# Backward chain of a segment-recurrent attention block: the order strings of a four-step block rewritten

## The chip, the cores and the metric

The kernel runs on one core of a Trainium2 chip. A core has five engines that run their own streams of instructions side by side: TensorE (PE; matrix products, its weight loads shown as PEld), VectorE (DVE), ScalarE (ACT), GpSimd (POOL) and SyncE (SP). Engines wait for each other on semaphores. DMA transfers are issued by SyncE and by GpSimd here, each on a queue of its own, and are carried out by 16 DMA engines. The metric is the device time of one execution in microseconds (us).

## The reference

```python
x = A_x
xn = _layernorm(x, axis=-1)
return x + _A_ref(xn, A_mem0, A_Wq, A_Wk, A_Wv, A_Wo, A_seg_len) + _B_ref(xn, ...)
```

`_B_ref` is a two-layer network with a squared ReLU (512 to 1792 to 512). `_A_ref` is attention with a recurrent memory: 2048 rows in 64 segments of 32, 32 heads of 128, and 8 memory rows that are put ahead of each segment:

```python
for s in range(n_seg):
    xs = x[:, s * seg_len:(s + 1) * seg_len, :].copy()
    h = jnp.concatenate([mem, xs], axis=1)
    q = jnp.einsum('btd,dhe->bhte', h, Wq)
    ...
    scores = jnp.einsum('bhqe,bhke->bhqk', q, k) * scale
    scores = jnp.where(mask[None, None], scores, -1000000000.0)
    p = _softmax(scores, axis=-1)
    o = jnp.einsum('bhqk,bhke->bhqe', p, v)
    o = jnp.einsum('bhte,hed->btd', o, Wo)
    mem = o[:, :M, :].copy()
    outs.append(o[:, M:, :])
```

The kernel returns this output and, for a given gradient of it, the gradients of x, of the first memory and of all weights and biases: `_out, _vjp = jax.vjp(_f, ...)`, then `_vjp(grad_out)`. Since the memory of a segment is the first 8 rows of the one before, both directions are chains of 64 steps. What can be computed for all segments at once is done ahead of the chains or behind them.

## The kernel before

The stages follow one another: the network B and the projections that need no memory (to about 265 us), the forward chain (to about 1110), the backward work on the memory's rows that can be done together (to about 1350), the backward chain (to about 2310), and the weights' gradients. The diff touches only the backward chain, L1150 to L1174.

**A step of the backward chain.** Step by step from the last segment to the first, the gradient of the memory, GT, comes in and the gradient for the segment before goes out. In the names of the order strings, with 0 and 1 (or a and b) for the two halves of the heads:

- `o0mm`, `o1mm`: products of GT with Wo (L425); `o0ev`, `o1ev`: ScalarE copies to gON; `o0fl`, `o1fl`: transposes on TensorE (L166); `o0te`, `o1te`: VectorE copies to gOT.
- `vp`: products for the gradient of v (L1381, L1383), copied by `vea`, `veb` (rows of the segment, gv) and `vla`, `vlb` (memory rows, b_gvL). `s0`, `s1`: the scores' gradients (L470), whose softmax backward is `d1` to `d4` on VectorE, ending in gS (L588); `tu` transposes it to gST (L488).
- `kp` (from gS with b_qN and b_qNL) and `qp` (from gST with b_kN and b_kNL), both L629, write the same PSUM banks b_pp, half 0 and half 1 in banks of their own. Their copies are `kea`, `keb` into gk, `qea`, `qeb` into gq, `kla`, `klb` into b_gkL. `vp` and the tile b_T of the step's end use b_pp too.
- `vg`, `kg`, `qg`: products of these copies with Wv, Wk, Wq (L498), 16 matrix products each, summed in ps_gR. `ra` (ScalarE) and `rb` (VectorE) copy the sum to R, `ta`, `tb` transpose it (L534), `Ha`, `Hb` reduce it to the next GT and `xa`, `xb` to b_XT (L543).

**A block.** Four steps are a block (128 rows), and 16 blocks make the chain. What is done once a block has the prefix `L.`: loads of the next block's memory rows (`ldv`, `ldk`, `ldt`, `lq`, `gl`), the left products `G`, `H`, `I` (L1248, 8 matrix products each, twelve a block) that turn the memory rows' gradients, and the stores. The large ones are six of 512 KB, gv, gk and gq in two halves each: `vo0`, `vo1`, `ko0`, `ko1`, `qo0`, `qo1`, all from L1235 to S_GB. `sx`, `sl`, `gst`, `vst`, `kst`, `qst` are smaller ones, and `vtr`, `ktr`, `qtr`, `L.vtr`, `gs` transposing DMAs. The tiles G4 of gv, gk, gq have one buffer: a copy of the next block's step into such a tile waits until the store has read it.

**Who issues.** SyncE issues the stores, the transposing DMAs and the two halves `ldk0`, `ldk1` of b_kNL (L1334; they do something only once a block). GpSimd issues `ldp` (b_P, L1324), `ldq` (b_qN, L1331), `ldn` (b_kN, L1332), `ldv`, `ldk`, and between them copies the probabilities into PD (`pb`, L1329) and b_vl into b_vT (`vc`, L1343). Loads and `pb`, `vc`, `vtr` serve the step after the one in which they are named.

**The order.** It is written out by hand. `B_ORDER` has four strings, rows 0 to 3, one for each step of a block, and `play` walks through them block after block:

```python
k = nm.rstrip("+-")
lag = nm.count("-") - nm.count("+")
if k.startswith("L."):
    b = n - 1 - lag
...
    s = n * SPB + j - lag
    if 0 <= s < NSEG:
        steps[step(s)][k]()
```

A name with four plus signs belongs to the step of its row, with three to the step before, with five to the one after. `L.` names with one plus belong to the block just finished or under way, with two to the next, without one to the one before. Each engine executes its share of the names in the order in which they stand. Which engine makes which copy is set by `ENGS` (L1175): ScalarE makes `kea0`, `keb0`, `keb1`, `kla0`, `kla1`, `qea0`, `qea1`, `qeb0`, `ra` and the copies of o and v, VectorE `kea1`, `klb0`, `klb1`, `qeb1` and the gOT copies.

Large stores and loads near the block's boundary stand on SyncE in the order `vo0 vo1 ldk0 ldk1 ko0 qo0 qo1 sx vtr ko1`, all in row 0.

Of the kernel before, what the change touches and what calls it, by code (L numbers as in the profile page):

```python
# [26 lines left out]
def kernel(  # L27
# [35 lines left out]
    L = M + SEG  # L63
# [145 lines left out]
    with sb("p1b", 2) as p1b, sb("p1", 1) as p1:  # L209
# [90 lines left out]
        for rb in range(NRB):  # L300
# [38 lines left out]
            xb = xq[rb]  # L339
# [314 lines left out]
    def on_engines(act, vec):  # L654

        return dict([(n, acp) for n in act.split()] + [(n, vcp) for n in vec.split()])
# [332 lines left out]
    with sb("la", 2) as la, sb("ls", 2) as ls, sb("lo", 1) as lo_, sb("wg", 2) as wg, psum("lpp", 1) as lpp, psum("lr", 4) as lr:  # L989
# [158 lines left out]


    B_ORDER = (  # L1150
# [6 lines left out]
        "pb+++ rb+++ ldq+++ L.H2+ ta+++ tb+++ vc+++ Ha+++ Hb+++ o0mm++++ o0ev++++ o1mm++++ o1ev++++ xb+++ o0fl++++ "  # L1157
# [4 lines left out]
        "ra++++ L.G3+ rb++++ ta++++ Ha++++",  # L1162
# [5 lines left out]
        "ta++++ rb++++ Ha++++ tb++++ Hb++++",  # L1168
# [5 lines left out]
        "ta++++ L.qst+ kla1++++ tb++++ L.H0++ Ha++++ Hb++++")  # L1174
    ENGS = on_engines(  # L1175
        "L.ra0 kea0 keb0 keb1 kla0 kla1 o0ev o1ev qea0 qea1 qeb0 ra vea veb vla vlb",
        "kea1 klb0 klb1 o0te o1te qeb1")
# [499 lines left out]
```

## Time and profile before

| | |
|---|---|
| time, median of 3 runs | 2895.26 us (2886.53 to 2903.46) |
| the profiled execution's own time | 2894.31 us |
| its span, first to last instruction | 2892.5 us |
| mean granted TensorE clock | 0.975 |
| busy: PE / PEld / DVE / ACT / POOL | 93% / 50% / 44% / 35% / 23% of the span |
| DMA | 586.62 MB, mean 203 GB/s |

Each group of instructions in the profile has its line, engine, operation, the tile written and the tile read, how often it ran, its busy time and mean duration in ns, and behind the bar the idle time of the engine just ahead of it with what ended it ("releaser"). L numbers are lines of the kernel. "SPq" and "POOLq" are the times in which SyncE or GpSimd issued a DMA. The chain of waits is followed back from the last instruction to what released it at each step. "issue" is time in which an engine waited for nothing that the profile shows. In views by stretches, PEclk is the clock that the throttle granted to TensorE (1.00 is full speed), and the DMA share is the mean busy share of the 16 DMA engines.

### The profile page before, as it was taken

What the parts mean: (1) busy time and instruction counts of PE and PEld (TensorE: products, weight loads), DVE (VectorE), ACT (ScalarE), POOL (GpSimd) and SP (SyncE); (2) the same over time, 40 slices, a digit from 0 to 9 for tenths busy, and PEclk for the clock granted to TensorE, in tenths of its full rate; (3) what the DMA queues carried; (4) which work ended last, traced back from release to release, by engine and by line L of the source; (5) the groups of instructions that cost most, each with busy time, mean ns of one, the idle gap of its engine ahead of it and who ended that gap; (6) DMA issues with size and microseconds to landing.
All of it is one profiled execution on the core that took longest, in us unless ns stands there. A gap on an engine that the chain in (4) does not pass through costs nothing.

```text
span 2892.5 us, 114613 instructions
## 1 busy us (share of the span) xinstructions
PE 2677.7 (93%) x51115; PEld 1444.8 (50%) x51252; DVE 1277.4 (44%) x3754; ACT 1003.8 (35%) x2330; POOL 658.9 (23%) x1279
## 2 busy tenths in 40 slices
PE   7998999999999887988999889998989899999999
PEld 3444555555555555455555445554544444444444
DVE  4543566666665664443545445544544401000000
ACT  2323444444454445332433333333333301111111
POOL 1000000000000001223434333343334334322221
PEclk9998999999999999998999999999999999999999
DMA  9766599999999888987568867776777799999993
GB/s 251 262 203 171 133 218 205 223 218 220 222 213 209 205 207 202 273 240 196 155 171 199 200 162 177 174 221 170 175 164 178 246 285 228 203 201 236 202 212 82
DMA packets 841920, 586.62 MB, mean 203 GB/s; under 512 B 639713, under 2 KB 729330, under 8 KB 838098
## 3 DMA queue, kind: packets, MB, share of 16 engines
q1 hardware_dynamic: 800370, 455.50, 69.6%
q0 software_dynamic: 41056, 123.77, 14.8%
q8 instruction: 402, 6.59, 1.0%
q14 instruction: 92, 0.75, 0.1%
HBM read 184.95 MB, written 248.79 MB: 150 GB/s over the span
## 4 chain that ended last, share of the span: by engine, by line
PE 72%; DMA 9%; SPq 8%; DVE 5%; issue 4%; ACT 2%; POOL 0%; DVEq 0%; ACTq 0%; POOLq 0%
PE ps_proj L425 15%; PE ps_gw L1638 12%; PE ps_gR L498 11%; PE ps_R L498 5%; SPq L1518 4%; PE ps_tr L166 3%; PE ps_RL L1248 3%; PE b_pp L629 3%; PE ps_L L383 3%; DMA S_GB<-gk 2%; PE ps_sc L470 2%; PE ps_B L344 2%; PE ps_gxb L353 2%; PE f_pp L629 2%; PE f_T L534 2%
## 5 line engine op out<-in xcount | busy, mean ns | idle before, releaser
L1638 PE MATMUL ps_gw<-gn,HNc 128*128 128x512 bf16 x1883 | 416.5, 380 | 6.9 <-issue 3.2
L1638 PEld LDWEIGHTS <-HNc 128*128 128x128 bf16 x1920 | 188.1, 98 | 230.0 <-issue 7.7
L407 ACT CAST f_N<-ps_proj 128x512 bf16<-128x512 f32 x320 | 183.8, 581 | 200.7 <-PE ps_proj L425 183.7
L1571 ACT CAST wt<-ps_gw 128x512 bf16<-128x512 f32 x128 | 74.4, 587 | 450.0 <-PE ps_gw L1638 416.6
L425 PEld LDWEIGHTS <-X 128*32 128x32 bf16 x5760 | 143.1, 96 | 136.7 <-DVE X L543 21.1
L1554 DVE TENSOR_TENSOR gx<-ps_rows,gb 128x512 f32<-128x512 f32 x16 | 11.1, 691 | 429.2 <-PE ps_rows L1552 400.6
L887 POOL COPY kM<-f_kT 128x256 bf16<-128x256 bf16 x64 | 25.7, 402 | 738.0 <-DVE f_kT L410 563.4
L498 PE MATMUL ps_gR<-Wv,gv 128*32 128x512 bf16 x2048 | 143.9, 401 | 3.8 <-issue 3.8
L498 PE MATMUL ps_gR<-Wk,gk 128*32 128x512 bf16 (+1 forms) x2048 | 139.8, 384 | 6.4 <-DVE gk L410 4.6
L1638 PE MATMUL ps_gw<-GOc,gn 128*128 128x512 bf16 x626 | 138.4, 379 | 5.1 <-ACT wt L1571 3.1
L498 PE MATMUL ps_R<-Wo,OT 128*32 128x256 bf16 x4096 | 131.3, 282 | 1.3 <-DVE OT L410 1.1
L498 PE MATMUL ps_gR<-Wq,gq 128*32 128x512 bf16 (+1 forms) x2048 | 125.6, 357 | 6.3 <-issue 6.3
L407 ACT CAST gON<-ps_proj 128x512 bf16<-128x512 f32 x128 | 75.0, 586 | 158.0 <-PE ps_proj L425 158.0
L425 PE MATMUL ps_proj<-Wq,X 128*32 128x512 bf16 x1920 | 126.8, 380 | 1.4 <-issue 0.8
L425 PE MATMUL ps_proj<-Wo,GT 128*32 128x512 bf16 x2048 | 123.4, 382 | 3.9 <-DVE GT L1293 3.6
L1572 POOL DMA_DIRECT2D out_dram<-wt x120 | 64.8, 542 | 271.0 <-ACT wt L1571 258.1
L407 ACT CAST gk<-b_pp 128x256 bf16<-128x256 f32 x192 | 69.2, 379 | 165.2 <-PE b_pp L629 94.0
L425 PE MATMUL ps_proj<-Wk,X 128*32 128x512 bf16 x1920 | 124.4, 381 | 1.9 <-issue 1.3
L425 PE MATMUL ps_proj<-Wv,X 128*32 128x512 bf16 x1920 | 121.5, 378 | 0.0
L1324 POOL DMA_DIRECT2D b_P<-S_A x63 | 33.8, 537 | 378.2 <-issue 137.4
L1329 POOL COPY PD<-b_P 32x320 bf16<-32x320 bf16 x256 | 115.3, 451 | 8.6
L498 PEld LDWEIGHTS <-OT 128*32 128x32 bf16 x4096 | 106.8, 99 | 8.9 <-DVE OT L410 1.3
(285 smaller groups left out, 5266.4 us busy)
## 6 DMA issues: line engine op xcount, KB each, us to landing
S_A<-f_N SPq DMA_DIRECT2D x64, 512.0 KB
out_dram<-wt POOLq DMA_DIRECT2D x134, 128.0 KB, 5.3
S_A<-f_N SPq DMA_DIRECT2D x64, 256.0 KB
S_GB<-gv SPq DMA_DIRECT2D x32, 512.0 KB
S_GB<-gk SPq DMA_DIRECT2D x32, 512.0 KB
S_GB<-gq SPq DMA_DIRECT2D x32, 512.0 KB
b_kN<-S_A POOLq DMA_DIRECT2D x63, 256.0 KB, 4.5
b_qN<-S_A POOLq DMA_DIRECT2D x63, 256.0 KB, 3.7
```

Source lines behind the costliest of these rows:

```text
L166: nc.tensor.transpose(ps_ap, in_ap, ident[base:base + k, base:base + k])
L383: nc.tensor.matmul(ps[:], lhsT=x(dc), rhs=Wqkv[t][:, dc, c0:c0 + 512], start=(dc == 0), stop=(dc == DC - 1))
L407: nc.scalar.copy(out, in_)
L425: nc.tensor.matmul(o, lhsT=hT[:, dc, :], rhs=x, start=(dc == 0), stop=(dc == DC - 1), tile_position=(0, 32 * g))
L498: nc.tensor.matmul(R[32 * g:32 * g + 32, 0:(cs.stop - cs.start) * P].rearrange("p (a b) -> p a b", b=P), lhsT=XT(k, g), rhs=x[:, cs, :], s ...
L629: nc.tensor.matmul(o, lhsT=N_[32 * g:32 * g + m, kk * P:(kk + 1) * P], rhs=X(kk)[32 * g:32 * g + m], start=(i == 0), stop=(i == len(jobs) ...
L1248: nc.tensor.matmul(ps["R", i][32 * g:32 * g + 32, :].rearrange("p (a b) -> p a b", b=P), lhsT=B_[n][:, k, g, :], rhs=W(g * KH + k), start= ...
L1329: nc.gpsimd.tensor_copy(PD[32 * g:32 * g + 32, g], C["P"][32 * g:32 * g + 32, :, KW - L:KW])
L1518: nc.sync.dma_start_transpose(got[i][q][:, x, :].rearrange("p (k e) -> p k e", k=KH), S_GB[4 * q + x, t][:, g].rearrange("p k r -> p (k r)"))
L1571: nc.scalar.copy(wt[:], ps[:])
L1572: eng(dst, wt[:])
L1638: nc.tensor.matmul(ps[:], lhsT=l(rc), rhs=r(rc), start=(n == 0), stop=(n == RC_ALL - 1))
```

## The change

All four strings of `B_ORDER` are rewritten. The set of names and the engine of each copy are the same. On SyncE, the order of a block becomes `vo0 qo0` (end of row 3), `gst vo1 ko1 ko0 vtr ldk0 ktr ldk1 qo1` (row 0), `vtr sl kst sx` (row 1), `vtr L.vtr gs vst gl qtr ldt` (row 2), `vtr qst lq` (row 3). On GpSimd `ldq` for a block's first step moves to the end of row 3. Products, copies and reductions stand in other places too. TensorE's order in row 2, for example, is `kp0 vg1 qp0 I3 kg0 kp1 qp1 qg0 kg1 qg1 H3 ta tb` before and `kp0 qp0 vg1 kg0 kp1 qg0 qp1 kg1 qg1 ta` after.

```diff
--- before.py
+++ after.py
@@ -1148,30 +1148,30 @@
 
 
     B_ORDER = (
-        "L.vo0+ o0mm++++ o1mm++++ L.vo1+ o0ev++++ pb+++ xa+++ L.xt ldk0+++ o1ev++++ o0fl++++ xb+++ L.ra0+ vp0++++ "
-        "o0te++++ L.G2+ ldk1+++ vea++++ s0++++ d10++++ o1fl++++ d20++++ L.ko0+ d30++++ vla++++ o1te++++ vp1++++ "
-        "ldn+++ L.I1+ L.G1+ d40++++ ldp++++ ldq+++ veb++++ s1++++ d11++++ vlb++++ kp0++++ ldp+++++ vg1++++ L.qo0+ "
-        "tu0++++ L.qo1+ keb0++++ d21++++ qp0++++ kla0++++ L.sx+ vg0++++ kea0++++ d31++++ qeb0++++ d41++++ vtr++++ "
-        "L.ko1+ kg0++++ klb0++++ tu1++++ qp1++++ ldn++++ qeb1++++ qea0++++ qg0++++ qea1++++ kp1++++ qg1++++ keb1++++ "
-        "kea1++++ kg1++++ klb1++++ kla1++++ ra++++",
-        "pb+++ rb+++ ldq+++ L.H2+ ta+++ tb+++ vc+++ Ha+++ Hb+++ o0mm++++ o0ev++++ o1mm++++ o1ev++++ xb+++ o0fl++++ "
-        "vp0++++ xa+++ o0te++++ vla++++ s0++++ o1fl++++ vp1++++ d10++++ vea++++ vtr++++ d20++++ L.H1+ o1te++++ L.ktr+ "
-        "d30++++ d40++++ veb++++ vlb++++ tu0++++ vtr+++++ s1++++ d11++++ d21++++ ldp+++++ d31++++ vg0++++ kp0++++ "
-        "qp0++++ d41++++ vg1++++ qea0++++ qeb0++++ qg0++++ keb0++++ L.kst+ tu1++++ kla0++++ klb0++++ kp1++++ kea0++++ "
-        "kea1++++ kg0++++ qp1++++ keb1++++ kla1++++ qeb1++++ L.ra1+ L.I2+ kg1++++ qea1++++ L.ra2+ qg1++++ klb1++++ "
-        "ra++++ L.G3+ rb++++ ta++++ Ha++++",
-        "vc+++ tb+++ Hb+++ ldq+++ o0mm++++ xb+++ o1mm++++ o0ev++++ o0fl++++ pb+++ xa+++ o1ev++++ o0te++++ vp0++++ "
-        "s0++++ d10++++ vea++++ d20++++ o1fl++++ L.vtr+ vp1++++ o1te++++ vg0++++ vla++++ s1++++ d30++++ d40++++ "
-        "d11++++ L.sl ldn+++ veb++++ tu0++++ d21++++ vlb++++ kp0++++ keb0++++ vg1++++ d31++++ d41++++ L.vst+ L.gs+ "
-        "kea0++++ qp0++++ tu1++++ qea0++++ klb0++++ kla0++++ L.I3+ kg0++++ qeb0++++ kp1++++ L.gl++ qp1++++ ldp+++++ "
-        "qea1++++ kea1++++ keb1++++ qeb1++++ qg0++++ klb1++++ kla1++++ L.gst+ kg1++++ ldq++++ qg1++++ ra++++ L.H3+ "
-        "ta++++ rb++++ Ha++++ tb++++ Hb++++",
-        "o0mm++++ o1mm++++ o0ev++++ vc+++ L.ra3+ ldn+++ xb+++ vtr++++ o1ev++++ xa+++ L.ldt++ o0fl++++ pb+++ vp0++++ "
-        "vc++++ o1fl++++ o0te++++ s0++++ vea++++ vla++++ o1te++++ d10++++ d20++++ vp1++++ s1++++ d30++++ veb++++ "
-        "vlb++++ d40++++ d11++++ vg0++++ kp0++++ L.tb+ kla0++++ tu0++++ d21++++ qp0++++ vg1++++ d31++++ keb0++++ "
-        "d41++++ kea0++++ kg0++++ kp1++++ L.qtr+ qeb0++++ tu1++++ L.G0++ klb0++++ qp1++++ L.ldv++ L.ta+ qea0++++ "
-        "qg0++++ qeb1++++ kea1++++ keb1++++ qea1++++ kg1++++ L.lq++ klb1++++ qg1++++ L.I0++ ra++++ L.ldk++ rb++++ "
-        "ta++++ L.qst+ kla1++++ tb++++ L.H0++ Ha++++ Hb++++")
+        "L.xt o0mm++++ o1mm++++ ldn+++ L.G2+ o0ev++++ xb+++ o1ev++++ o0fl++++ L.gst vp0++++ L.vo1+ L.ko1+ xa+++ "
+        "o0te++++ vc+++ vp1++++ o1fl++++ veb++++ L.ko0+ s0++++ vtr++++ o1te++++ d10++++ L.H0+ L.H2+ ldk0+++ vla++++ "
+        "d20++++ vea++++ d30++++ vg1++++ d40++++ s1++++ d11++++ kp0++++ vg0++++ tu0++++ vlb++++ qp0++++ L.ra0+ "
+        "kla0++++ klb0++++ d21++++ L.ktr+ d31++++ keb0++++ ldk1+++ d41++++ vc++++ kea0++++ L.I2+ ldp++++ L.qo1+ "
+        "kg0++++ ldn++++ L.I1+ qeb0++++ qea0++++ tu1++++ qp1++++ qea1++++ qg0++++ qeb1++++ kp1++++ keb1++++ kea1++++ "
+        "kla1++++ qg1++++ kg1++++ ra++++ klb1++++",
+        "L.G1+ pb+++ ldq+++ rb+++ ta+++ Ha+++ tb+++ Hb+++ ldp++++ o0mm++++ o0ev++++ vtr++++ xa+++ o1mm++++ xb+++ "
+        "o0fl++++ o1ev++++ vp0++++ o0te++++ L.H1+ s0++++ vea++++ d10++++ o1fl++++ vp1++++ o1te++++ veb++++ vg0++++ "
+        "vc++++ d20++++ vla++++ vlb++++ s1++++ d30++++ d40++++ tu0++++ L.sl kp0++++ d11++++ qp0++++ d21++++ vg1++++ "
+        "kla0++++ kea0++++ qea0++++ L.kst+ d31++++ qeb0++++ L.G3+ d41++++ L.ra1+ tu1++++ keb0++++ L.I3+ qg0++++ "
+        "qp1++++ kp1++++ kg0++++ qea1++++ klb0++++ keb1++++ L.sx+ kla1++++ kea1++++ ldq++++ klb1++++ L.ra2+ qeb1++++ "
+        "kg1++++ qg1++++ ra++++ L.H3+ ta++++",
+        "rb+++ pb+++ Ha+++ tb+++ Hb+++ ldn+++ xa+++ vtr++++ o0mm++++ o1mm++++ xb+++ L.vtr+ L.ra3+ L.gs+ o0ev++++ "
+        "o0fl++++ o0te++++ L.vst+ o1ev++++ vp0++++ s0++++ d10++++ ldp++++ d20++++ o1fl++++ d30++++ vla++++ vea++++ "
+        "o1te++++ vp1++++ d40++++ tu0++++ vlb++++ vg0++++ s1++++ veb++++ vc++++ ldp+++++ d11++++ kp0++++ kea0++++ "
+        "klb0++++ qp0++++ kla0++++ d21++++ d31++++ qeb0++++ vg1++++ keb0++++ qea0++++ d41++++ tu1++++ kg0++++ L.gl++ "
+        "kp1++++ L.qtr+ qg0++++ kla1++++ qp1++++ L.ldt++ ldq++++ keb1++++ kea1++++ kg1++++ qeb1++++ qea1++++ qg1++++ "
+        "klb1++++ ldn++++ ra++++ ta++++ rb++++",
+        "tb+++ Ha+++ Hb+++ o0mm++++ xb+++ o0ev++++ vtr++++ xa+++ o1mm++++ pb+++ vp0++++ o0fl++++ o1ev++++ o1fl++++ "
+        "vea++++ o0te++++ s0++++ L.qst+ vla++++ o1te++++ vp1++++ d10++++ d20++++ d30++++ s1++++ d40++++ vg0++++ "
+        "vlb++++ tu0++++ L.lq++ veb++++ kp0++++ L.vo0++ qp0++++ qea0++++ d11++++ klb0++++ keb0++++ qeb0++++ kea0++++ "
+        "d21++++ kla0++++ L.G0++ d31++++ d41++++ vg1++++ L.ta+ L.ldv++ kp1++++ kg0++++ kea1++++ pb++++ kla1++++ "
+        "qg0++++ keb1++++ tu1++++ qp1++++ klb1++++ L.ldk++ qea1++++ kg1++++ qeb1++++ qg1++++ L.I0++ ldq++++ ra++++ "
+        "ta++++ rb++++ L.qo0++ L.tb+ Ha++++ tb++++ Hb++++")
     ENGS = on_engines(
         "L.ra0 kea0 keb0 keb1 kla0 kla1 o0ev o1ev qea0 qea1 qeb0 ra vea veb vla vlb",
         "kea1 klb0 klb1 o0te o1te qeb1")
```

## The prediction

> **What bounds the kernel now.** I read the chain of waits by engine first, then the backward chain's step times, then its waits, then one block's queues. In the page's chain:
>
> ```profile
> PE 72%; DMA 9%; SPq 8%; DVE 5%; issue 4%; ACT 2%; POOL 0%; DVEq 0%; ACTq 0%; POOLq 0%
> ```
>
> TensorE is the bound wherever it isn't kept waiting. The edit changes only the backward chain; the tile GT, whose last reduction ends a step, dates it, and a view by stretches shows one block and the first step of the next:
>
> ```profile
> L543 DVE TENSOR_REDUCE GT<-b_T x120: 223/225/226, 1400.9 to 2277.6; 128x16 bf16<-128x64 f32 x120
> ...
> core 0: us, PE busy (x) PEld busy (x) DVE busy (x) ACT busy (x) POOL busy (x), PEclk, DMA share, GB/s
> 1829.20:1847.90 18.70, 15.80 (x373) 8.13 (x374) 7.31 (x26) 6.03 (x16) 5.19 (x11) 0.91 0.87 256
> 1847.90:1860.90 13.00, 12.88 (x357) 7.14 (x357) 7.88 (x23) 5.35 (x15) 4.68 (x9) 1.00 0.60 112
> 1860.90:1873.90 13.00, 12.81 (x350) 7.06 (x349) 6.32 (x21) 5.63 (x15) 4.48 (x9) 1.00 0.70 134
> 1887.90:1905.50 17.60, 14.07 (x373) 7.58 (x373) 7.26 (x25) 6.13 (x16) 5.70 (x12) 1.00 0.97 307
> 1400.90:2277.60 876.70, 801.37 (x21074) 435.26 (x21078) 427.57 (x1341) 332.24 (x900) 335.07 (x652) 0.97 0.75 184
> ```
>
> Two reductions a step make 60 steps, 876.7/60 = 14.6 us each. The two middle rows are steps without disturbance: 13.00 us, TensorE busy for 12.88 and 12.81. Anything that stops TensorE there lengthens the step by as much. The rows of 18.70 and 17.60 are the first steps of a block, over which the DMA share is 0.87 and 0.97. Over the whole stretch TensorE stands for 876.7 - 801.4 = 75 us, and a mean clock of 0.97 is worth another 0.03 x 877 = 26 us. The waits of this stretch (us in total, times, longest) name a part of that:
>
> ```profile
> PE b_pp L629 <- issue: 27.7, 21, 3.9
> ACT gk L407 <- DMA S_GB<-gk: 25.2, 11, 3.3
> PE ps_gR L498 <- issue: 11.2, 12, 1.8
> PE b_pp L629 <- DMA b_qN<-S_A: 10.9, 8, 2.8
> DVE gk L410 <- DMA S_GB<-gk: 10.8, 5, 2.8
> PE b_pp L629 <- DVE gS L588: 8.8, 10, 1.7
> ```
>
> Two things there hang on the order of the DMA issues: products that wait for qN, and copies into gk that wait until a store has read it. "Issue", TensorE waiting for nothing recorded, is larger than both.
>
> **Where the burst stands.** SyncE's own queue at that block's end, one GpSimd load, and the TensorE row that waits for it:
>
> ```profile
> 1823.61 0.95 SPq L1235 DMA_DIRECT2D S_GB<-gv  x2
> 1825.41 1.75 SPq L1334 DMA_DIRECT2D b_kNL<-S_NL  x2
> 1827.60 1.27 SPq L1235 DMA_DIRECT2D S_GB<-gk  x1
> 1828.92 1.72 SPq L1235 DMA_DIRECT2D S_GB<-gq  x2
> ...
> 1833.79 3.80 SPq L1338 DMA_TRANSPOSE b_vl<-S_A  x1
> 1837.65 0.59 SPq L1235 DMA_DIRECT2D S_GB<-gk  x1
> ...
> 1828.99 0.54 POOL L1331 DMA_DIRECT2D b_qN<-S_A  x1
> ...
> 1835.86 0.20 PE L629 MATMUL b_pp<-gS,b_qN 32*128 32x40 bf16 x4 [0.71 <-DMA b_qN<-S_A]
> ```
>
> Five of the six stores go out in 7 us around the step's start at 1829.2, the sixth 8.5 us after it. The load of qN, issued among them, is needed 6.9 us later and is late. The sixth, the second half of gk, is the one that step 0's copies into gk wait for. The chain of waits has these landings (start, us) on it:
>
> ```profile
> 1586.44 9.64 DMA S_GB<-gk
> 1655.79 6.20 DMA S_GB<-gk
> 1828.99 6.82 DMA b_qN<-S_A
> 2321.87 18.20 DMA S_GM<-b_GN
> ```
>
> **The change, part by part.** Nothing is removed or added: the same instructions in another order. But although it is told as a move of DMA issues, the strings also put products, copies and reductions in another order on TensorE, ScalarE and VectorE.
>
> (a) Stores and qN. In the changed kernel vo0 goes out behind veb of row 3, qo0 at its end, vo1, ko1, ko0 during the Wo products of row 0, qo1 some 4 us into it. Counted back from the step's start by the middle rows' 13 us, that is about -7, -5.5, -5, -3.5, -2.5 and +4: again five stores in about 6 us. I leave the "issue" waits as they are (bounds: 27.7 + 11.2 = 38.9 us gone; or half as much again, +19). What improves is the tail of the burst: ko1 leaves 10 us earlier, so the copies find gk free, and qN's issue stands at the end of row 3 instead of behind kN and P in row 0, 3 to 4 us earlier against a lateness of at most 2.8. The qN wait is worth 10.9 us. Of the copies' wait on gk only what reached TensorE counts:
>
> ```profile
> L498 PE MATMUL ps_gR<-Wk,gk 128*32 128x512 bf16 (+1 forms) x1920 | 130.2, 382 | 6.2 <-DVE gk L410 4.6 <-issue 1.1
> L629 PE MATMUL b_pp<-gS,b_qN 32*128 32x40 bf16 x1920 | 43.6, 178 | 24.5 <-DMA b_qN<-S_A 10.9 <-DVE gS L588 8.8 <-issue 3.2
> ```
>
> 4.6 us on the products, to which I add an equal 4.5 for their weight loads behind the same copies (bounds 0 and the 10.8 of VectorE's wait). The sum is 20 us saved. These waits are 20 of TensorE's 75 us of standing, so I credit them the same share of the clock's 26 us: 7 us. Together -27 us (bounds -15 without those loads and the clock, -52 with all of both).
>
> (b) kNL. Its two halves stand in row 0 now, behind vo1, ko1, ko0 and the transpose on SyncE's queue: first half about +0.5 to +3 us after the step's start, where it was -3.8. The product qp0 of step 0 needs it: kp0 started at 6.66 - 0.71 = +6.0 of its step, vg1 now stands ahead of it too (0.87, below), and kp0's 0.3 and vg0's 0.87 come between: about +8. No row prices this load; qN's 6.82 us under the same burst is nearest, and a store's 9.64 bounds it above. It then lands between +7.3 and +9.8, up to 1.8 us late, with qp0 and all behind it on TensorE waiting. I take 0.7 us a block, 15 blocks, +10.5 us (bounds 0; and a store's landing from +1, 2.5 us each, 37).
>
> The Trainium skill ("DMA: Bandwidth & Descriptors", section "Queues, rings and completion order") says that every DMA engine takes turns packet by packet between queue rows, while one row's ring is consumed in order. That speaks against moving kNL behind the stores on their own queue, whereas qN, on GpSimd's, shares turns with them. By that rule the upper bound would be nearer; no row here shows a load behind three stores.
>
> (c) The order of products and copies. These rows price it, with a quiet step's product of 16 and a left product of 8 (their starts are 0.87 and 0.54 us before the next row's), and the copy that follows the end of a product at 1845.18 by 0.18:
>
> ```profile
> L407 ACT CAST gk<-b_pp 128x256 bf16<-128x256 f32 x180 | 64.8, 379 | 151.5 <-PE b_pp L629 85.9 <-DVE gq L410 40.3 <-DMA S_GB<-gk 25.2
> L407 ACT CAST b_gkL<-b_pp 128x64 bf16<-128x64 f32 x120 | 26.2, 218 | 48.3 <-PE b_pp L629 43.5 <-DVE gk L410 3.2
> L410 DVE CAST gk<-b_pp 128x256 bf16<-128x256 f32 x60 | 25.3, 422 | 72.5 <-ACT gq L407 32.2 <-PE b_pp L629 29.5 <-DMA S_GB<-gk 10.8
> L488 DVE STREAM_TRANSPOSE gST<-gS 128x256 bf16<-128x256 bf16 x120 | 52.7, 439 | 2.1
> L407 ACT COPY R<-ps_gR 128x512 f32<-128x512 f32 x61 | 35.8, 587 | 87.0 <-PE ps_gR L498 87.0
> ...
> 1844.82 0.20 PE L629 MATMUL b_pp<-gS,b_qN 32*128 32x40 bf16 x4
> ...
> 1845.01 0.17 PE L629 MATMUL b_pp<-b_GL,b_qNL 32*128 32x16 bf16 x4
> 1845.12 1.05 PE L498 MATMUL ps_gR<-Wq,gq 128*32 128x512 bf16 x16
> 1845.99 0.61 PE L498 MATMUL ps_gR<-Wk,gk 128*32 128x256 bf16 x16
> 1846.86 0.60 PE L1248 MATMUL ps_RL<-Wk,b_gkL 128*32 128x512 bf16 x8
> 1847.40 0.85 PE L534 MATMUL b_T<-identF,R 128*128 128x128 f32 x4
> ...
> 1845.36 0.37 ACT L407 CAST gk<-b_pp 128x256 bf16<-128x256 f32 x1 [1.85 <-PE b_pp L629]
> ```
>
> Six places lose their cover:
> - Row 0: kla0, keb0, kea0 all follow qp0 (keb0 stood ahead of it, vg0 behind it). 0.18 + 0.22 + 0.38 + 0.38 = 1.16 before kg0, and only I2's 0.54 between: 0.6.
> - Row 1: kg1 needs kea1, which on VectorE follows ScalarE's qea1 and keb1 into the same tile: 0.18 + 0.38 + 0.38 + 0.42 = 1.36, kg0 covers 0.87: 0.5.
> - Row 2: kea0 stands between kp0 and qp0, which writes the banks that it reads, and vg1 is no longer between: 0.18 + 0.38: 0.55.
> - Row 2: kg1 directly behind qp1, ahead of which keb1 can't run: 0.55.
> - Row 2's end: L.H3 (0.54) no longer stands between the last product and ta, which needs the copy R (0.18 + 0.59): 0.2 to 0.54, say 0.35.
> - Row 3: qp0 directly behind kp0, without L.tb between; gST takes 0.44, kp0 0.3 (1844.82 to 1845.12): 0.14, and some 0.1 for the signal: 0.25.
>
> That is 2.8 us a block. In rows 0 and 1 such a pause may coincide with an "issue" wait of the same step, so I count 2.5 x 15 = 37.5 us (bounds 1.0 and 2.8: 15 and 42). Left products have moved from rows 2 and 3 into rows 0 and 1; their sum stays. Other places change nothing I can price: each copy there has a product of 0.87 us behind it.
>
> (d) Behind the chain, gst of the last block stands later on SyncE's queue, and the landing at 2321.87 lies on the chain into the next stage: 0 to +3 us, taken as 0.
>
> The sum, from the profiled execution's 2894.3 us (0.03% under the median of 2895.26): 2894.3 - 27 + 10.5 + 37.5 = **2915 us**.
>
> **The rivals.**
> - *The forecast*: the order's pauses outweigh the landings saved. 2915 us, chance 0.35.
> - *Not slower: the burst goes early.* The stores leave while row 3's products run, so that row 0, where the two stretches of 17 to 19 us lie, loses half its "issue" waits and some clock. For it: DMA share 0.87 to 0.97 over just those steps. Against it: as many stores in as short a time. Price: -27, -19.5 for half of 38.9, -7 of clock, +23 for pauses of 1.5 us of which the rest fall into other waits: 2864 us. It decides once the waits on TensorE lose over 3.2 us a block, the 48 us of (b) and (c) over 15. Chance 0.26.
> - *It cancels*: pauses of 1.5 us a block (22.5), kNL late by 0.3 (4.5), -27: 2894 us. For it: 1.1 of the 2.8 lie in rows 0 and 1, where TensorE stands already. Chance 0.22.
> - *kNL lands behind the stores*: 2.5 us a block on qp0, with kg0 and qg0 queued behind it on TensorE: 2894.3 - 27 + 37.5 + 37.5 = 2942 us. For it, 9.64 us of a store's landing; against it, half the burst is over by then. Chance 0.17. The rule of the Trainium skill's DMA page cited above would bring this case.
>
> That the change doesn't do what it says belongs to the second and fourth: if the burst is as dense as before, "issue" is unchanged, and only the order counts.
>
> **How the numbers follow.** About 0.5% is what a measurement of this kernel can tell from no change: 2881 to 2910. The first and last cases are slower, 0.52; the third within, 0.22; the second faster, 0.26. The range runs from just under the second case to just over the last, 2858 to 2946, leaving about 0.1 beyond each end. The slower side's own range is 2905 to 2946.
>
> **What would show it.** Right: quiet steps of row 2 at 14 us or more, with TensorE waiting for gk on ScalarE and for R; no wait of L629 on qN; copies into gk that no longer wait for S_GB. A wait of L629 on kNL measures (b). Wrong: steps of rows 1 and 2 still at 13.0 us, which strikes out (c), or "issue" well under 39 us, which makes the second case. A faster result would mean that the burst's place, not TensorE's stream, set the time.

## The result, and the profile after

The changed kernel takes 2919.4 us (median of 10 runs, 2889.39 to 2922.82) against 2894.44 us (median of 10, 2886.53 to 2907.47): a ratio of 1.0066, 95% interval 1.0041 to 1.0090. Six of the ten runs of the changed kernel lie between 2918 and 2923 us and the four others between 2889 and 2909, so its median stands above its mean, 2912.8 us: the loss is 25 us by the medians, 18 by the means and 19 by the ratio. The forecast was 2915 us, and the median came out 4 us from it. The sum behind that number did not: the profile puts the loss in another stage than the forecast did.

The term for the order's pauses is there almost to the digit, and the landings that the forecast counted as saved are gone. Waits of the changed kernel in the backward chain, from 1400 to 2290 us (total, times, longest):

```profile
PE ps_gR L498 <- DVE gk L410: 16.9, 31, 0.7
PE b_pp L629 <- issue: 16.9, 15, 2.4
PE ps_gR L498 <- issue: 15.4, 16, 2.4
PE b_pp L629 <- ACT gk L407: 7.8, 15, 0.5
PE ps_gR L498 <- ACT gk L407: 7.0, 13, 0.6
PE b_T L534 <- ACT R L407: 4.5, 15, 0.3
PE b_pp L629 <- DMA b_kNL<-S_NL: 3.6, 3, 2.0
```

The four rows of gk and R are the pauses of the new order: 16.9 + 7.8 + 7.0 + 4.5 = 36.2 us. The row of 10.9 us for qN is gone, and so are the 25.2 and 10.8 us of copies waiting for the store of gk. A quiet row 2 (1867.20 to 1880.50), the pauses in brackets with what ended them:

```profile
1873.29 0.20 PE L629 MATMUL b_pp<-gST,b_kN 32*128 32x32 bf16 x4 [0.52 <-ACT gk L407]
1877.86 1.05 PE L498 MATMUL ps_gR<-Wk,gk 128*32 128x512 bf16 x16 [0.67 <-DVE gk L410]
1880.09 0.90 PE L534 MATMUL b_T<-identF,R 128*128 128x128 f32 x4 [0.31 <-ACT R L407]
```

That step lasts 13.30 us and TensorE is busy for 11.65 of them, where the quiet steps of before had 12.88 and 12.81 of 13.00: two left products (H3, I3) have moved from row 2 to row 1, which lasts 13.80 us.

The chain of 64 steps is no longer than before in this profile. Its first and last reduction into GT, before and then after, each with the same stretch in the view by stretches (length, then busy time of each engine, granted clock, DMA share, GB/s):

```profile
L543 DVE TENSOR_REDUCE GT<-b_T x126: 223/225/226, 1375.2 to 2290.5; 128x16 bf16<-128x64 f32 x126
...
1375.20:2290.50 915.30, 837.57 (x22086) 455.36 (x22090) 446.82 (x1403) 348.86 (x945) 349.19 (x680) 0.97 0.73 180
2290.50:2418.00 127.50, 118.09 (x907) 55.75 (x917) 16.93 (x47) 20.69 (x44) 43.87 (x73) 0.99 1.03 277
```

```profile
L543 DVE TENSOR_REDUCE GT<-b_T x126: 223/224/226, 1376.7 to 2292.6; 128x16 bf16<-128x64 f32 x126
...
1867.20:1880.50 13.30, 11.65 (x333) 6.72 (x332) 7.07 (x22) 5.63 (x15) 4.79 (x9) 1.00 0.79 158
1376.70:2292.60 915.90, 817.83 (x22086) 454.76 (x22090) 445.67 (x1404) 346.96 (x945) 352.15 (x679) 0.99 0.73 180
2292.60:2420.00 127.40, 97.40 (x778) 44.71 (x785) 13.06 (x40) 15.35 (x34) 33.67 (x56) 0.88 1.08 234
```

915.9 us against 915.3. TensorE runs the same 22086 recorded matrix products, stands 98.1 us in place of 77.7, and is busy 19.8 us less: the clock went from 0.97 to 0.99. In this pair of profiles the pauses were paid, and the clock gave back as much. Over three profiles each, with the runs below in which only gst or HNc is moved, TensorE stands 19 us longer and is busy 13 us less. The first step of this block, from 1835.40 to 1853.40 us, has a DMA share of 0.95, as high as before: five of the six large stores go out just ahead of its start, from 1826.08 to 1833.13.

What is lost lies behind the chain. From its end to the end of the span it is 602.0 us before (2892.5 - 2290.5) and 627.4 us after (2920.0 - 2292.6). In the last row of each fence, TensorE is busy for 118.1 of the first 127.5 us of that stage before, and for 97.4 of 127.4 after. TensorE there, before and then after:

```profile
2318.93 60.59 PE L1638 MATMUL ps_gw<-GOc,gn 128*128 128x512 bf16 x274 [1.28 <-DMA GOc<-in_grad_out_dram]
2382.62 17.43 PE L1638 MATMUL ps_gw<-GOc,gn 128*128 128x512 bf16 x78 [3.10 <-ACT wt L1571]
```

```profile
2319.06 32.75 PE L1638 MATMUL ps_gw<-GOc,gn 128*128 128x512 bf16 x148 [1.17 <-issue]
2361.66 7.77 PE L1638 MATMUL ps_gw<-GOc,gn 128*128 128x512 bf16 x23 [9.85 <-DMA GOc<-S_GM]
2376.45 24.91 PE L1638 MATMUL ps_gw<-GOc,gn 128*128 128x512 bf16 x103 [7.01 <-DMA gn<-S_OL]
```

The changed kernel waits 9.9 and 7.0 us for loads, and then 8.6 us more until a copy to wt frees a bank: 25.5 us in three stands, where the kernel before has one of 3.1. The chain of waits of the changed kernel goes through GpSimd's queue there (start, us):

```profile
2300.77 7.25 DMA S_GB<-gv
2308.15 0.75 POOL GOc L1586
2311.87 15.84 DMA GOc<-S_GM
...
2328.99 20.57 DMA gn<-S_ON
2349.84 26.47 DMA gn<-S_OL
```

GpSimd's first load of GOc from S_GM goes out at 2308.15, after a wait of 11.9 us; before, it went out at 2294.65. It reads what gst stores, and gst of the block before the last is now issued at 2300.02, among the large stores (2283.68 before). The releaser is given as the store of gv, the DMA that came last by the profile; S_GM's own is issued 0.8 us ahead of it. Behind the wait come loads of gn that take 20 to 26 us of the chain of waits. Over the same time SyncE runs the four transposing loads HNc. Before, then after (durations of the issue, then first and last start):

```profile
L1610 SPq DMA_TRANSPOSE HNc<-S_HT x4: 2686/10551/17044, 2340.8 to 2374.5; - x4
```

```profile
L1610 SPq DMA_TRANSPOSE HNc<-S_HT x4: 5062/16944/33290, 2327.6 to 2389.6; - x4
```

They start 13 us earlier, and their issues last until 2400, 72 us in place of 41. Two explanations offered themselves: the late store alone, or GpSimd's loads, made late by it, meeting the early transposing loads.

### The profile page after: what moved, and what is told of

It is laid out like the page before. It is cut to its first block, busy times and chain, and to the rows that moved or that the text cites. A ratio compares the mean times of both kernels' runs of the same rounds, so it can differ in the third digit from the quotient of the medians.

```text
span 2920.0 us, 114571 instructions
## 1 busy us (share of the span) xinstructions
PE 2660.9 (91%) x51115; PEld 1446.9 (50%) x51252; DVE 1275.5 (44%) x3754; ACT 1001.0 (34%) x2330; POOL 662.0 (23%) x1279
## 4 chain that ended last, share of the span: by engine, by line
PE 74%; DMA 9%; DVE 5%; SPq 5%; issue 4%; ACT 3%; POOL 0%; another core or an unknown queue 0%; ACTq 0%; DVEq 0%; POOLq 0%
PE ps_proj L425 15%; PE ps_gw L1638 13%; PE ps_gR L498 11%; PE ps_R L498 4%; SPq L1518 3%; PE b_pp L629 3%; PE ps_RL L1248 3%; PE ps_tr L166 3%; PE ps_L L383 2%; PE ps_sc L470 2%; DMA gn<-S_OL 2%; PE f_pp L629 2%; PE ps_B L344 2%; PE ps_w L1104 2%; PE b_T L534 2%
## 5 line engine op out<-in xcount | busy, mean ns | idle before, releaser
L887 POOL COPY kM<-f_kT 128x256 bf16<-128x256 bf16 x64 | 25.6, 401 | 744.4 <-DVE f_kT L410 570.6
L1638 PE MATMUL ps_gw<-GOc,gn 128*128 128x512 bf16 x626 | 145.7, 393 | 27.3 <-DMA GOc<-S_GM 9.8
L498 PE MATMUL ps_gR<-Wk,gk 128*32 128x512 bf16 (+1 forms) x2048 | 132.8, 373 | 31.3 <-DVE gk L410 17.3
L498 PE MATMUL ps_gR<-Wv,gv 128*32 128x512 bf16 x2048 | 136.3, 383 | 7.5 <-issue 5.6
L1343 POOL COPY b_vT<-b_vl 128x1024 bf16<-128x1024 bf16 x64 | 66.4, 1037 | 324.7 <-PE ps_sc L470 156.6
L1638 PEld LDWEIGHTS <-gn 128*128 128x128 bf16 x640 | 64.2, 100 | 107.3 <-issue 37.2
```

The lines of the kernel that those rows point to most:

```text
L498: nc.tensor.matmul(R[32 * g:32 * g + 32, 0:(cs.stop - cs.start) * P].rearrange("p (a b) -> p a b", b=P), lhsT=XT(k, g), rhs=x[:, cs, :], s ...
L1343: nc.gpsimd.tensor_copy(vT[:, :, :, MAIN], C["vl"][:])
L1638: nc.tensor.matmul(ps[:], lhsT=l(rc), rhs=r(rc), start=(n == 0), stop=(n == RC_ALL - 1))
```

## The experiments

Every kernel was compared with the kernel before, run on the same chip. In the experiments, 11 or 12 runs stand against 28 to 34. The ratios are set against the kernel before as it ran beside each experiment (medians 2895.5 to 2898.1 us); the medians of different rows are compared below only as a rough guide.

| kernel | median us | ratio, 95% interval | chain us | behind it us |
|---|---|---|---|---|
| before (first profile) | 2894.4 | | 915.3 | 602.0 |
| changed | 2919.4 | 1.0066 (1.0041 to 1.0090) | 915.9 | 627.4 |
| gst back | 2897.6 | 1.0018 (0.9996 to 1.0040) | 924.4 | 597.7 |
| before, gst late | 2896.4 | 1.0006 (0.9981 to 1.0030) | 914.5 | 604.3 |
| issues alone | 2890.3 | 0.9983 (0.9957 to 1.0008) | 907.6 | 610.3 |
| order alone | 2915.4 | 1.0071 (1.0045 to 1.0097) | 922.9 | 598.1 |
| changed, HNc held | 2905.2 | 1.0027 (1.0001 to 1.0053) | 916.7 | 603.3 |
| issues, kNL early | 2887.5 | 0.9966 (0.9942 to 0.9990) | 903.0 | 614.0 |
| the same, HNc held | 2878.3 | 0.9942 (0.9918 to 0.9966) | 897.5 | 600.7 |
| kNL behind qo0 | 2880.6 | 0.9940 (0.9915 to 0.9964) | 895.8 | 601.7 |
| stores early | 2874.3 | 0.9917 (0.9892 to 0.9942) | 891.9 | 601.6 |
| before, HNc held | 2901.0 | 1.0025 (0.9997 to 1.0053) | 909.7 | 602.3 |

The last two columns are from one profiled execution each (the GT rows, and the span). The kernel before has the chain 915.3, 914.5 and 909.7 us in three of them (the second with gst late, the third with HNc held, which leave the order on TensorE, ScalarE and VectorE as it is), the changed one 915.9, 924.4 and 916.7: 913 and 919 on average, so a difference of a few us there is within the scatter. So is the time to the chain's start, which was between 1371.6 and 1387.4 us with the same code ahead of it.

**gst put back.** The store of S_GM stands in row 2 again.

```diff
 row 0
-o0fl++++ L.gst vp0++++
+o0fl++++ vp0++++
 row 2
-L.gl++ kp1++++ L.qtr+
+L.gl++ kp1++++ L.gst+ L.qtr+
```

> The changed kernel with one DMA put back: gst, the store of GT's rows to S_GM, stands behind the GT load in row 2 again (the store of the block just finished) and no longer a block later in row 0. In the profile of the changed kernel the backward chain, from the first to the last reduction into GT, lasts 916.0 us against 915.3 before, and the 25 us lie behind it: GpSimd's load GOc from S_GM waits 11.9 us, and all its later loads stand behind it. Theory A (the late store of S_GM holds up the loads of the weight-gradient stage): the chain stays near 916, the wait of 11.9 us goes, the stage behind the chain falls from 627 to about 602 us, and the time to about 2896 us. Theory B (the transposing loads HNc, which SyncE starts 13 us earlier than before, collide with GpSimd's loads, whatever gst does): the stage stays near 627 us and the time near 2919. Theory C, the forecast as it stood (the chain itself lost 21 us and what lies behind it is noise): no change, 2919.

2897.6 us, and the stage behind the chain at 597.7 us: one DMA's place takes back 22 of the 25 us by the medians, and 14 of 19 by the ratios. GpSimd's first load of GOc goes out at 2306.5, 4.3 us behind the last reduction into GT, in place of 15.5. Theory C, the forecast's own, is out, and so is B in its strict form (whatever gst does). But HNc moved too: it starts 49.9 us after the last reduction here (2302.2 to 2352.1), 35.0 us in the changed kernel. So the late store and the collision were not told apart yet.

**gst late in the kernel before.**

```diff
 row 0
-o0fl++++ L.ra0+
+o0fl++++ L.gst L.ra0+
 row 2
-L.gl++ qp1++++ ldp+++++ qea1++++ kea1++++ keb1++++ qeb1++++ qg0++++ klb1++++ kla1++++ L.gst+ kg1++++
+L.gl++ qp1++++ ldp+++++ qea1++++ kea1++++ keb1++++ qeb1++++ qg0++++ klb1++++ kla1++++ kg1++++
```

> The kernel before with that one DMA moved the other way: gst from row 2 to row 0, a block later. Theory A: the chain stays at 915, the stage behind it grows from 602 to about 625 us, the time to about 2917 us. Theory B and C: nothing worth measuring, 2894 us, since the products' order and the burst of stores are those of before.

2896.4 us: theory A as put fails. The idle times ahead of GOc's rows in this kernel and of HNc:

```profile
  DMA S_GM<-b_GN: 18.8, 2
  ACT wt L1551: 4.7, 1
...
L1590 SPq DMA_TRANSPOSE HNc<-S_HT x4: 5132/11675/21254, 2337.4 to 2382.2; - x4
```

GpSimd waits for S_GM, 18.8 us in two waits (15.7 in one wait in the kernel before), and its first load of GOc goes out 16.3 us behind the last reduction, as late as in the changed kernel. But TensorE loses only 4.7 us, and HNc starts 43.4 us behind that reduction (2294.0 to 2337.4). The late store by itself is harmless here. It takes the early transposing loads as well.

**HNc held, in the changed kernel.** This tries just that: gst stays late, the transposing loads wait.

```diff
         loads(2)
+        pdma(side[0:1, 0, 0:64], S_XN[0:1, 0:64])
```

> The changed kernel, gst as it is there (late), but the four transposing loads HNc are held back: a small load on GpSimd's queue, behind the last of its first loads of gn, writes 64 elements of the tile HNc ahead of them, so that SyncE starts them when those loads have landed (about 2355 to 2365 us in place of 2327.6). The runs so far: gst back in the changed kernel gives 2897.6 us and removes both the 11.9 us wait of GOc and the early start of HNc (50 us behind the last GT reduction against 35); gst late in the kernel before gives GOc waits of 18.8 us, HNc at 43 us and only 2896.4 us. Theory A1 (the collision: the late store delays GpSimd's loads past the early HNc transposes, which then slow each other): with HNc held, loads of gn land in about 10 to 15 us and not 20 to 29, TensorE loses under 5 us behind the chain, and the time is about 2898 us. Theory A2 (the late GOc loads alone): the stage stays near 627 us and the time near 2919.

2905.2 us by the median. The stage behind the chain is 603.3 us, TensorE stands there for 1.2 and 3.4 us, and:

```profile
2321.86 60.59 PE L1619 MATMUL ps_gw<-GOc,gn 128*128 128x512 bf16 x274 [1.17 <-issue]
2385.81 19.11 PE L1619 MATMUL ps_gw<-GOc,gn 128*128 128x512 bf16 x78 [3.36 <-ACT wt L1551]
...
L1591 SPq DMA_TRANSPOSE HNc<-S_HT x4: 3020/3564/6745, 2375.6 to 2389.7; - x4
```

The product that was cut twice runs through for 60.6 us. The four transposing loads take 17 us once those loads of gn have landed, against 41 and 72 us beside them. A2 is out, A1 holds in kind; of the 22 us that gst put back recovers, 14 come back by the medians, and 11 by the ratios (1.0066 to 1.0027, whose intervals just overlap). The stage behind the chain, 24 us shorter in the profile, shows it more plainly. The control, the kernel before with the same line added:

> The control: the kernel before with nothing changed but HNc held. TensorE stands only 4.4 us in the stage behind the chain in the profile of before, so if the collision takes the changed kernel's late gst, this changes nothing worth measuring: 2890 to 2896 us. If HNc and GpSimd's loads cost each other time in every version: 5 to 10 us less, about 2887.

2901.0 us, ratio 1.0025, an interval that just takes in 1, and neither of the two expected times. With HNc held in both, the changed kernel and the one before are not told apart (1.0027 and 1.0025). So the hold by itself gives no gain where there is no collision, and may cost a few us, which is about what the held version of the changed kernel lacks. Why the changed kernel's HNc starts early (its wait for an earlier SyncE store ends sooner) was not tried by itself. That the single runs of the changed kernel scatter from 2889 to 2923 us would fit a collision that doesn't come about each time; it was not traced.

**The issues alone.** TensorE, ScalarE and VectorE in the order of before, the two queues in that of the changed kernel (gst as before). SyncE over a block:

```diff
-row 0: vo0 vo1 ldk0 ldk1 ko0 qo0 qo1 sx vtr ko1   row 1: vtr ktr vtr kst
-row 2: L.vtr sl vst gs gl gst                      row 3: vtr ldt qtr lq qst
+row 0: vo1 ko1 ko0 vtr ldk0 ktr ldk1 qo1           row 1: vtr sl kst sx
+row 2: vtr L.vtr gs vst gl gst qtr ldt             row 3: vtr qst lq vo0 qo0
```

> The order of TensorE, ScalarE and VectorE of the kernel before, with the DMA issues of the changed one (and gst as before, so that the stage behind the chain doesn't decide). By the view that the chain's equal length hides two terms of opposite sign, the pauses of the order (about 2.5 us a block, 37 us) and what the issues save: the chain falls from 915 to about 880 us and the time to about 2858 us. By the forecast's terms (landings and clock -27, kNL +10.5): 2878 us. If the spread of the issues only shifts the stalls: 2894 us.

2890.3 us: 12 us above the forecast's terms, and 32 us above what the first view expected. Its waits, and its stretch of the chain:

```profile
PE b_pp L629 <- DMA b_kNL<-S_NL: 16.0, 11, 2.3
...
1383.30:2290.90 907.60, 839.66 (x22086) 457.56 (x22090) 443.86 (x1404) 348.44 (x945) 351.40 (x678) 0.97 0.77 182
```

qN is never waited for, but kNL now is, in 11 of 15 blocks for 16.0 us: it takes the place of qN. The clock stays at 0.97. The ratio, 0.9983, is not clear of no change: in this profile the spread of the issues trades one late landing for another.

**The order alone**: the changed kernel's order on the three engines, both queues as before.

> The other half: the changed kernel's order of TensorE, ScalarE and VectorE with the DMA issues of the kernel before, on both queues. If the order's pauses add to the old stalls: the chain grows by about 37 us to 952, the time to about 2931 us. If the pauses fall into stalls that are there anyway (no instruction to run, loads landing late): the chain stays near 915 to 925 and the time near 2894 to 2905.

```profile
PE ps_gR L498 <- DVE gk L410: 15.7, 29, 0.7
PE b_pp L629 <- ACT gk L407: 7.8, 15, 0.5
PE ps_gR L498 <- ACT gk L407: 6.9, 13, 0.6
PE b_pp L629 <- DMA b_qN<-S_A: 1.9, 3, 1.0
...
1386.30:2309.20 922.90, 819.59 (x22086) 455.34 (x22090) 452.52 (x1404) 346.98 (x945) 350.86 (x677) 0.99 0.70 179
```

2915.4 us, between the two expectations. The pauses are the same, but the wait for qN falls from 10.9 to 1.9 us with the issues where they were: a step that pauses gives its loads more time. TensorE stands for 103.3 us, 25.6 more than before, and is busy 18.0 us less, at a clock of 0.99. The medians say 20 us for this half. Its one profile shows 8 of them in the chain, and the scatter of the time ahead of it is as large as the rest. With the new order in place the moved issues are worth more than alone: from this kernel to the one with gst put back, which differs from it in the two queues, the ratio falls from 1.0071 to 1.0018, some 15 us.

**kNL early.** The issues-alone kernel, with the two loads right behind qp1 of row 3.

```diff
 row 0
-ldk0+++ ldk1+++
 row 3
-qp1++++ L.ta+ qea0++++
+qp1++++ L.ta+ ldk0++++ ldk1++++ qea0++++
```

> The issues-alone kernel (2890.3 us, of which the profile shows 16.0 us of TensorE waiting for kNL in 11 blocks, and 12 stretches at half clock, 5 of them behind such waits) with the two halves of kNL moved ahead of the stores: behind qp of row 3, right after the product that frees the tile. If kNL's place behind the stores on SyncE's queue is what the wait comes from: the wait goes to 0 to 2 us, and with the clock behind it the chain is 20 to 25 us shorter, about 2868 us. If the load is late because the DMA engines are full in any place: 2885 to 2890 us.

TensorE waits no more for kNL, so the load was late by its place on the queue. But the time is 2887.5 us instead of 2868: SyncE now waits at kNL for qp1, and the stores behind it are late.

```profile
SPq L1314 <- PE b_pp L629: 80.4, 15, 7.1
...
DVE b_XT L543 <- DMA S_XG<-b_XT: 23.4, 11, 2.6
```

In this profile TensorE also stands 12.0 us behind the chain, with HNc at its usual place beside GpSimd's loads. With HNc held too:

> The same with HNc held back as well. If the collision behind the chain is a matter of the late gst alone, this adds nothing over the kernel with kNL early (within 5 us). If HNc and GpSimd's loads also slow each other when both start at the usual place (the issues-alone profile has 610 us behind the chain against 602 before): some 5 to 8 us less.

2878.3 us, 9 us less, with intervals that overlap (0.9942 to 0.9990, and 0.9918 to 0.9966). The stage is 600.7 us long, in place of 614.0, without that stand. So in these profiles the collision is not the late gst's alone, and gst's place is one thing that decides how much the two sets of loads meet; in the kernel before, at the same usual place, it cost TensorE 3.1 us.

**kNL behind qo0**, where qp1 is over, and S_XG's store at row 0's transposing load.

```diff
 row 0
-vtr++++
+vtr++++ L.sx+
 row 1
-L.ra1+ L.I2+ L.sx+ ldq++++
+L.ra1+ L.I2+ ldq++++
 row 3
-L.ta+ ldk0++++ ldk1++++ qea0++++
+L.ta+ qea0++++
-L.qo0++ tb++++
+L.qo0++ ldk0++++ ldk1++++ tb++++
```

> The version with kNL early and HNc held (2878.3 us), mended where its profile shows new waits: SyncE stood 80 us in 15 blocks with kNL at the head of its queue (waiting for the product that frees its tile), the stores behind it left late, and VectorE's b_XT waited 23 us for the store S_XG. Here kNL goes behind qo0 at the end of row 3, when that product is over, and S_XG's store right behind the transposing load of row 0. If the blocked queue cost what the new waits show (TensorE standing 5.5 us for b_gvL and 9.2 us for b_XT): both go, kNL stays under 3 us, and the time falls by some 12 us to about 2866. If kNL behind one store is late again: a wait of 5 to 10 us on kNL and no gain, 2878.

2880.6 us, no gain by the median, though b_XT's wait is gone; the chain is 895.8 us in place of 897.5. The wait for b_gvL went from 5.5 to 3.5 us. The new waits were not what limited it.

**Stores early**, in addition vo1 and ko0.

```diff
 row 0
-L.vo1+ vea++++
+vea++++
-L.ko0+ vp1++++
+vp1++++
 row 3
-L.vo0++ qp0++++
+L.vo0++ L.vo1++ qp0++++
-kea0++++ L.ldv++
+kea0++++ L.ko0++ L.ldv++
```

> The same with two more of the large stores moved ahead: vo1 directly behind vo0, and ko0 as soon as the last copy into its half is issued, both in row 3; ko1 and qo1 stay in row 0. If the stall around the block's end follows from stores landing late in row 0 (gv, gk still being read): waits of ScalarE on S_GB go from some 20 us to under 8, about 2862 us. If the number of bytes in the burst sets the stalls (TensorE without an instruction to run, 35 to 45 us in every profile so far): no change against the version before, within 5 us.

2874.3 us, a ratio of 0.9917 (0.9892 to 0.9942): faster than both kernels of this study. It is 6 us below the version before it, which the two intervals don't tell apart, and short of the 2862 us expected. Its waits, over the chain:

```profile
PE b_pp L629 <- issue: 24.3, 22, 3.2
PE ps_gR L498 <- issue: 17.0, 15, 2.3
...
1371.80:2263.70 891.90, 831.62 (x22086) 454.11 (x22090) 444.06 (x1403) 348.26 (x945) 350.91 (x678) 0.98 0.74 185
```

Copies into gq wait 5 us for stores. TensorE stands for 60.3 us, and 41 of them are "issue" on b_pp and ps_gR, which no placement tried here has lowered below 28.

## Why the prediction was right or wrong

The number and the sign were right, the composition was not: the chain was to lose 21 us and what lies behind it nothing. In the profile the chain loses 1 us (a mean of 6 over three executions each) and the stage behind it 25.4. That the chain lost 20 us less than forecast, and that 25 us were lost behind it where the forecast had nothing, cancelled by luck.

- *The order's pauses (c), 37.5 us*: right. They measure 36.2 us, and place by place 0.52, 0.67 and 0.31 us in row 2 (0.55, 0.55 and 0.35 worked out), 31 waits for VectorE's gk (the places in rows 1 and 2), 15 for ScalarE's ahead of qp0 (row 2), 13 ahead of a product (row 0). Nothing of L629 waiting for gST in row 3 shows in the waits: the 0.25 there did not come. Of the signs named for it, the waits came, but not a row 2 of 14 us or more: it lasts 13.30 us, since the row also gives up two left products.
- *The landings saved (a), -20 us*: right in kind; the waits for qN and for the store of gk are gone, and "issue" on b_pp and ps_gR stays, 38.9 us to 32.3, as assumed. But the order-alone kernel shows that the pauses would have removed most of the wait for qN without any issue moved.
- *The clock (a), -7 us*: this is the term of the chain that was mis-sized. The clock went from 0.97 to 0.99 and TensorE's busy time fell by 19.8 us. The forecast gave the clock to the landings by their share of the standing time, but it goes with the order: 0.99 in the order-alone kernel, 0.97 in the issues-alone one. The size differs between executions: in the chain TensorE is busy for 818 to 827 us in the four profiles with the new order, and for 833 to 840 in the four with the old order and kNL behind stores. That the pauses replaced some of the long stands, which cost clock (below), fits this and was not tried by itself.
- *kNL (b), +10.5 us*: 3.6 us, in 3 blocks. Its first half went out 2.5 us behind a step's start (1837.85), as worked out. Without the pauses it was 16.0 us in 11 blocks, so its size was guessed well for a kernel that doesn't exist, and too high for the one with the new order. The Trainium skill ("DMA: Bandwidth & Descriptors", "Queues, rings and completion order") has one row's ring consumed in order. The runs agree: kNL behind three stores is waited for (16.0 us), ahead of them it isn't, though there it is issued earlier too. The upper bound of 37 us was not reached.
- *The stands for gS, 8.8 us*, were left in the sum and don't appear among the changed kernel's larger waits: another gain that was not counted. They are there with the order alone (9.9 us) and not with the issues alone.
- *What lies behind the chain (d), 0 to +3 us*: this is the step that failed. The forecast looked at the landing of the last block's S_GM, at 2321.87, which lies on the chain of before, and priced gst's later place by it. It didn't ask which load waits for the S_GM of the block before the last, nor what stands behind that load on GpSimd's queue, nor what else starts meanwhile. 22 of the 25 us go when gst goes back, by the medians.
- *The rivals*: the second (burst early, half of the "issue" gone) did not happen: "issue" fell by 6.6 of 38.9 us. The third, that it cancels, describes the chain, with 2894 us forecast and 2897.6 us measured once gst is put back, though by other terms than it named. The range, 2858 to 2946, held the time.

## What to carry to other kernels

When an order is rewritten, follow each moved store to its reader, in the next stage too, and each reader's queue to whatever stands behind it: the largest cost here began with a store that nothing in its own stage waits for. Pauses in a stream that loses time to late landings anyway did not simply add here: the wait for qN fell from 10.9 to 1.9 us with the order alone. Where two halves of a change can be run alone, run them: equal totals hid +36 us and as much of the opposite sign.

## What the runs showed of the hardware

TensorE's clock fell behind stands that are shorter than the stretch for which it then runs at half rate. In the kernel before, a stand of 1.51 us, with the 3.4 us around it and the 3.4 us that follow:

```profile
2001.44 0.83 PE L498 MATMUL ps_gR<-Wq,gq 128*32 128x512 bf16 x12 [1.51 <-issue]
...
1998.90:2002.30 3.40, 1.89 (x58) 0.97 (x58) 0.98 (x3) 0.70 (x2) 3.28 (x8) 1.00 1.03 389
2002.30:2005.70 3.40, 3.40 (x52) 1.99 (x48) 0.04 (x1) 0.70 (x2) 1.00 (x2) 0.50 0.93 276
```

The clock record in the traces has 12 such stretches in the chain of before, each of 3.41 or 6.83 us, 51 us in all, and 3 in that of the changed kernel, 10 us; half the difference, 20 us, is what TensorE's busy time fell by. The fall goes with how much of such a stretch TensorE is busy, not with the length of one stand. Over the chains of all twelve kernels, cut in step with these stretches, the 106 falls to half rate came behind stretches of 3.41 us with at most 2.17 us busy, and no stretch with less than 1.55 us busy was left without one. Between the two it went either way: from 1893.10, a stand of 1.69 us with 1.71 us busy had no fall behind it. The three pauses of 0.31 to 0.67 us in the changed kernel's row 2 left the clock at 1.00 (the row of 13.30 us). The Trainium skill ("TensorE: Matmul & The Clock Gate", "Part 1: The HAM clock gate") gives an idle window of about 3.4 us as what closes the gate; here 1.5 us of standing, in a stretch of 3.4 us that was 1.89 us busy, was followed by half rate.

The traces show what may lie behind the stands that the profile puts to "issue". The DMA queue named "instruction" moves 168 blocks of 16 KB between 1400 and 2290 us of the kernel before. In the chains of six kernels (before, changed, gst back, issues alone, order alone, stores early) there are 133 such stands of TensorE of 0.8 us or more, and every one of them ends 1.20 to 1.65 us after one of these blocks has been moved; for moments taken at random that time is mostly between 0.5 and 5 us. So TensorE seems to wait there for its own instructions, which share the DMA engines with the loads and stores. No kernel here tried this by itself.

The four transposing loads took 17 to 22 us in the five kernels in which they were held, 41 to 50 us beside loads of GpSimd's queue, and 72 us where they met all of these at their start. The loads of gn that were issued from 2330 to 2360 us took 25.2 us (1 MB) and 27.5 us (256 KB) in that last case, by the median, and 15.7 and 13.8 us in the kernel before.
